# Sums of squares of the first expert's weights on TensorE, the last chunk's operands kept on chip, and a new sequence

## The chip, the cores and the metric

One core of a Trainium2 chip runs the whole program: TensorE (PE) with its weight loads (PEld), VectorE (DVE), ScalarE (ACT), GpSimd (POOL), and SyncE (SP), which issues nearly all DMAs. The metric is the device time of one execution in microseconds (us).

## What is computed

Causal attention with a decay bias over 4 x 8 heads, 576 positions of 64 elements, then two feed-forward stages ("experts") over the 2304 tokens:

```
scores = q k^T / 8 + min(-(cum_i - cum_j), 0), masked;  attn = softmax(scores) v
x  = attn, heads side by side                     # 2304 x 512
h  = x @ w_in;  x = (h - tanh(h)) @ w_out          # 512 -> 2048 -> 512
y  = ((x @ w_a) * (x @ w_b)) @ w_out2              # 512 -> 1536 -> 512
```

All inputs and the output are float32.

## The kernel before

**Split products.** PE multiplies float16. A float32 matrix is scaled by a power of two and split into a high and a low float16 half; a product of two matrices is three float16 products (high-high, high-low, low-high). The power of two comes from the sum of squares of the matrix: an ACT Square over the tile with an accumulator gives one sum per partition (tile `wac`), a matmul with a 128x128 matrix of ones (`ones16`) adds them over the partitions into a one-column result in the PSUM bank `pv`, and five tiny DVE instructions (`pow2`, first of them `p2n`) turn that into the scale `wsc` and its inverse. Then the high half is made by a scaled copy (`copy_scaled`, on any of ACT, DVE, POOL) and the low half by a multiply and subtract (`lo_part`, on DVE or POOL). `w_split` (L902) does all this for one weight tile of 128 x 1024.

**First expert.** Its weights lie in `w1`: 8 chunks of 256 hidden columns, each an in-tile and an out-tile, so 16 tiles. Tokens go through in nine blocks of 256. Block 0 runs with the float32 weights, as they are fetched; `w_split` then turns each of the 16 tiles into halves in place, and blocks 1 to 8 use the split weights. Attention units (two heads of one batch, part of the positions) run on the same engines, ahead of the block that needs them.

**Second expert.** Its 18 weight tiles are fetched and split when the last attention unit is done (their Square stays on ACT in both kernels). Tokens go in blocks of 512. From the second on, sums of quarters of the matrices save one product in eight: `seven` for the two inner products, and in the last three blocks `four_act`, `four_mm`, `four_out` for the outer one. `four_act` makes the operands of both halves (l = 0 and l = 1) of a block from one chunk c of six; those of l = 1 are stored to DRAM (`pb_d`, from the tile `sq`, tag sq4, one buffer) and loaded again (tile `x2f`, two buffers) when `four_mm` for l = 1 multiplies them. In the last block the chunks 4 and 5 of l = 1 are plain: no sums, into two banks of their own (`blk["plain"]`). `four_out(l)` combines the four accumulators of a half by copies and adds; for the last block's l = 1 it is called before those two plain chunks, and `plain_out` adds their result and stores the rows. `four_out` for both halves uses the tile `th`, of which there is one, and `g`, of which there are two.

**What sets the order.** Operations are recorded with their operands. The string `ORDER` then lists every operation in the order in which it is issued, three characters each: the operation's number and which of its possible engines takes it. Each engine executes its share strictly in that order and waits by semaphores for operands and buffers. A changed number of operations needs a new string, and the new one puts all operations in another order.

Of the kernel before, what the change touches and what calls it, by code (L numbers as in the profile page):

```python
# [37 lines left out]
    "AAMAAEAB0AAIAAQAAUAAAAAYABsAB4ABoABwAAcAAgAAkAAsAAwAA0ABEABJABNABSAAoAA4AA8ABAABVABZABkACEACAAB8ACIACMACQACYAQQAIkACUACc"  # L38
    "ACgAF0ADAAC0AFsACkAQUADKACwAIoAI0ADMAQYABgAIYAIUAIcADEAIgAIsAF9ACoAC4AFwADRAIwAF4ABcADUAPIAGAAPEAQcAPNAY4AI4AI8AJAAC8AQA"
    "AJIADYAJEAFoAY8AJMAJ4AJQACtADdAJwAPRAPUADgAJ8ADsAiAAJ1AEgAJUAEsAqEAKEAMcADkADoADwAPwAD0AEkAZAAMgAMkAD4AD8AEwAGEAhwAEoAJs"  # L40
    "AE0AERAEUAGKAMpAHMAHQAMwAiEAh4AGMAEYAEAAEcAE4AEEAE8AFCAJYAJdAGYAFRAFFAPYAZEAFUAGQAJgAGcAHUAEIAFYAFdAHYAHcAZMAFIAQEAKOAEM"
    "AFNAFgAMYAQIAGUAGgAQMAGkAKJAGoAHgAHkAG9APcAPkAYUAh0AHoAPsAGuAPgAH8AP0AGwAHAAHuAG0AZIAHEAh8AKBAHwAG5AHIAKQAKUAKYAKcAKgAH0"
    "AKkAJmAIAALQAFkAMuAM1AKoAQgALcAIEAP4AIIAYYAiQAKsAKyAM6AM8ALBAH5ALEAP8ALIAXwAK0ALgANIAJpALUALYALkANAARAANEAQwARQAlcAYcANM"
    "ANQALMAX0AX4AX8ALoAYgALsALyAK4AYAAK8AMBANUAYEAZQAL0AMEAIMANYANeAIRANtAN8AL4AL9AYIANwAOAAMIAiMAOIANhAUQAPoANkAYOAMMAiIAN0"
    "AYkAOEAjIAiUAOMAOQANpAiYAicAUYAikAigAOUAQkAN4AioAixAOYAMQAOeAOtAisAYoATwAOwAO0Ai9AOgAOkAQoAMVAlqAT4AO5AOoAO8AliAjAAQsAjV"
# [103 lines left out]
    "EVQEV8EUwEWcEKpEWgEVFEWBEWFEWwEWIEKsEVIEW8EWoEWMEVUEXAEYoEW0EVZEWQETMEYAEYIEVcEW4EWsEXEEXJEYMEYwEXNEXQEXVEVgEYsEZEEYFEXq"  # L149
    "EXsEYQEVkEXZEXwEXcEYgEY0EY8EYkEXiEY5EZIEZMEbUEZQEYcEZUEbMEbcEbIEYVEYZEbYEZBEXkEZYEZ9EbQEbgEVoEZcEZlEZtEZxEZpEZhEZ0EZ4EaB"  # L150
    "EX4EX8EX0EbkEbsEboEbwEb0EaIEb4EaMEb8EaZEcAEaVEcsEcwEc0EaQEaEEc4Ec8EdAEacEahEapEasEakEa1Ea4EawEa8EbAEcEEcNEcIEcREcZEcgEcU"
    "EccEcoEdYEdcEdhEclEdIEdNEdQ"
# [1895 lines left out]
```

## Time and profile before

| | us |
|---|---|
| three runs, median (lowest to highest) | 931.09 (930.62 to 933.18) |
| profiled execution, device time | 930.71 |
| its span, first to last instruction | 928.9 |
| DMA, whole span | 123.38 MB, 133 GB/s in the mean |

A busy share is an average over stages with different limits, so the rows below cut the span into stretches. "Idle" of an engine in a stretch is its length less the busy time. A timeline row begins with start and duration; a row with xN merges N instructions, from the first start to the last end; "[0.70 <-ACT qk]" says how long the engine stood idle before and what released it. Matmuls overlap in the array, so one takes longer than the distance to the next.

### The profile page before, as it was taken

The numbers are of one execution on the slowest core, as the hardware profiler recorded it, in microseconds if no ns is written. First come the engines' busy times: TensorE is split into PE (matmuls) and PEld (weight loads), VectorE is DVE, ScalarE is ACT, GpSimd is POOL, SyncE is SP. The second block draws the span as 40 slices with busy tenths as digits, with TensorE's granted clock in tenths as the row PEclk, the third lists the DMA queues.
The fourth block names the chain that finished last, engine by engine and source line by source line (L and its number), as shares of the span: only waits on it lengthen the run. The fifth ranks groups of instructions, "written<-read, shape, count | busy, mean of one in ns | idle before, by whom it ended". The sixth has DMA issues, their size and how long they took to land.

```text
span 928.9 us, 20616 instructions
## 1 busy us (share of the span) xinstructions
PE 881.3 (95%) x7650; PEld 647.6 (70%) x7650; DVE 805.7 (87%) x2011; ACT 574.1 (62%) x1136; POOL 346.1 (37%) x495
## 2 busy tenths in 40 slices
PE   1798899999999999999899999999999999999996
PEld 1565576766666666567566677777778888888884
DVE  8999999789999899997999999989798749864764
ACT  6999998668889888974998544433333323421310
POOL 2523356344544654552222310143322342344342
PEclk9999999999999999999999999999999999999998
DMA  8979976668999998975866300300211161123223
GB/s 204 304 214 238 231 123 124 113 154 171 206 165 174 193 179 167 208 137 161 308 206 189 84 24 1 69 2 1 47 54 53 60 185 65 62 72 112 72 68 115
DMA packets 260197, 123.38 MB, mean 133 GB/s; under 512 B 228544, under 2 KB 236976, under 8 KB 260096
## 3 DMA queue, kind: packets, MB, share of 16 engines
q1 hardware_dynamic: 259936, 121.79, 55.6%
q8 instruction: 60, 0.98, 0.4%
q14 instruction: 41, 0.34, 0.1%
q10 hardware_dynamic: 160, 0.26, 0.1%
HBM read 63.67 MB, written 19.03 MB: 89 GB/s over the span
## 4 chain that ended last, share of the span: by engine, by line
PE 47%; DVE 5%; issue 2%; DMA 1%; POOL 1%; ACT 0%; SPq 0%; POOLq 0%; DVEq 0%; ACTq 0%
PE h L647 16%; PE qk L647 12%; PE acc L647 11%; PE pv L647 8%; DVE w L647 1%; DVE x2f L647 1%; DVE g L647 1%; DMA x2f<-pb_d 0%; DMA out_dram<-x2f 0%; DVE a L647 0%; DVE ghl L647 0%; DVE sq L647 0%; DVE xf L647 0%; DVE h L647 0%; DVE th L647 0%
## 5 line engine op out<-in xcount | busy, mean ns | idle before, releaser
L647 PEld LDWEIGHTS <-w 128*128 128x128 f16 x3840 | 372.2, 98 | 67.0 <-issue 4.0
L647 PE MATMUL h<-xhl,w 128*128 128x256 f16 x2256 | 276.9, 273 | 2.4 <-DVE ghl L647 1.1
L647 PE MATMUL acc<-w,ghl 128*128 128x512 f16 (+1 forms) x1092 | 233.6, 358 | 0.9 <-DVE sq L647 0.9
L647 PEld LDWEIGHTS <-ghl 128*128 128x128 f16 x1290 | 123.6, 98 | 99.9 <-issue 4.8
L647 PE MATMUL h<-xf,w 128*128 128x256 f16 (+1 forms) x416 | 71.3, 310 | 0.0
L647 DVE CUSTOM_DVE_ANT_0 qk<-qk,caus,cs 128x384 f32<-128x384 f32 (+3 forms) x120 | 64.9, 555 | 2.8 <-PE qk L647 1.4
L647 PE MATMUL qk<-xf,w 128*128 128x256 f16 x432 | 55.2, 273 | 0.8 <-DVE xf L647 0.6
L647 PE MATMUL pv<-xf,w 128*128 128x256 f16 x432 | 55.0, 273 | 0.0
L647 ACT ACTIVATE g<-h 128x512 f32<-128x512 f32 x40 | 23.4, 592 | 48.8 <-PE h L647 27.0
L647 ACT ACTIVATE w<-w 128x1024 f32<-128x1024 f32 (+1 forms) x45 | 50.9, 1156 | 1.4 <-DVE w L647 1.4
L647 ACT ACTIVATE th<-h,xc 128x512 f32<-128x512 f32 x64 | 43.7, 683 | 9.5 <-PE h L647 7.4
L647 PE MATMUL qk<-qkT 128*128 128x128 f16 (+4 forms) x168 | 45.7, 316 | 3.7 <-ACT zs L647 3.1
L647 PE MATMUL qk<-kB,qB 67*128 67x128 f16 (+4 forms) x168 | 45.3, 313 | 3.9 <-ACT zs L647 2.2
L647 PEld LDWEIGHTS <-v 128*64 128x64 f16 x1440 | 37.7, 113 | 12.8 <-issue 10.8
L647 PEld LDWEIGHTS <-x2f 128*128 128x128 f16 x360 | 35.1, 98 | 7.1 <-DMA x2f<-pb_d 0.8
L647 DVE SCALAR_TENSOR_TENSOR h<-h,xc,th 128x512 f32<-128x512 f32 x48 | 36.0, 751 | 1.6 <-ACT th L647 1.6
L647 ACT ACTIVATE zs<-qk,nm 128x128 f32<-128x128 f32 (+1 forms) x64 | 30.2, 472 | 11.2 <-DVE nm L647 9.4
L647 DVE SCALAR_TENSOR_TENSOR ghl<-h,xsg,ghl 128x512 f16<-128x512 f32 x48 | 35.8, 746 | 1.4 <-ACT ghl L647 0.9
L647 DVE SCALAR_TENSOR_TENSOR a<-qk,sm,a 128x512 f16<-128x512 f32 (+1 forms) x56 | 35.2, 630 | 1.4 <-ACT a L647 1.0
L647 ACT ACTIVATE qk<-qk,nm 128x512 f32<-128x512 f32 (+1 forms) x56 | 31.7, 566 | 7.4 <-DVE nm L647 5.4
L647 ACT ACTIVATE sq<-qk 128x512 f32<-128x512 f32 x22 | 13.1, 594 | 37.4 <-PE qk L647 35.0
L647 PE MATMUL pv<-aT,v 128*64 128x128 f16 x960 | 34.5, 225 | 1.3 <-DVE aT L647 0.8
(367 smaller groups left out, 1872.0 us busy)
## 6 DMA issues: line engine op xcount, KB each, us to landing
w<-in_moe_w_out_dram SPq DMA_DIRECT2D x8, 1024.0 KB
pb_d<-sq SPq DMA_DIRECT2D x16, 448.0 KB
x2f<-pb_d SPq DMA_DIRECT2D x16, 448.0 KB
w<-in_moe_w_in_dram SPq DMA_DIRECT2D x6, 1024.0 KB
x_d<-sq SPq DMA_DIRECT2D x9, 512.0 KB
w<-in_moe_w_a_dram SPq DMA_DIRECT2D x4, 1024.0 KB
out_dram<-x2f SPq DMA_DIRECT2D x16, 256.0 KB
ws<-in_moe_w_out_dram SPq DMA_DIRECT2D x3, 1024.0 KB
```

The costliest lines, as they stand in the source:

```text
L647: return getattr(getattr(plan.nc, name), what)(*[real(a) for a in args], **{k: real(a) for k, a in kw.items()})
```

## The change

1. `w_split` takes a new path for the 16 tiles of the first expert (`GRAMS = 16`). The upper 16 bits of each float32 weight are read as bfloat16 (every second element). Eight matmuls of such a 128x128 piece with itself add up in PSUM to a 128x128 matrix, whose diagonal holds the sums of squares. One DVE instruction multiplies that by the identity `eyeh` and accumulates each row into `wac`. The matmul with ones then goes into a column of the same bank beside it. The ACT Square is gone for these tiles.
2. For the last chunk (c = 5) of the last block the operands of l = 1 are neither stored nor loaded; `four_mm` takes them from the tile where `four_act` wrote them.
3. `four_out` for the last block's l = 1 uses a free place in `w1` in place of `th` and `g`, makes the products `yy` of the two output scales itself and scales by them in one copy on any engine; `plain_out` reuses `yy`.
4. A new `ORDER`.

```
 ORDER = (
-    "AAMAAEAB0AAIAAQAAUAAAAAYABsAB4ABoABwAAcAAgAAkAAsAAwAA0ABEABJABNABSAAoAA4AA8ABAABVABZABkACEACAAB8ACIACMACQACYAQQAIkACUACc"
+    "ABkAB0AAAAAEAAIABwABoAB4AAQAB8AAMAAUAAYABsAAcAAgACAAAkAAsAAwAA0ABEABJABNAAoABRAA4ABVABaAQQAA8ABAACEACIACMAIoAIUACQACYACc"
...
+GRAMS = 16
...
+    def gram(flat, acc, g):
+        x = flat.bitcast(BF16)[:, 1::2]
+        n = flat.shape[1] // P
+        with pl.group():
+            for i in range(n):
+                y = x[:, i * P:(i + 1) * P]
+                pl.tensor.matmul(g, y, y, start=(i == 0), stop=(i == n - 1), skip_group_check=True)
+        pl.vector.tensor_tensor_reduce(
+            out=g, in0=g, in1=eyeh, scale=1.0, scalar=0.0, op0=ALU.mult, op1=ALU.add, accum_out=acc)
+
     def w_split(wf, dst, inv, junk):
...
-        pl.scalar.activation(out=junk, in_=wf, func=AF.Square, accum_out=acc)
         tot = bank("pv")
-        pl.tensor.matmul(tot[:, :1], ones16, acc.bitcast(BF16)[:, 1:2], start=True, stop=True)
-        pow2(tot[:, :1], 1, inv, sc)
+        if junk is None:
+            gram(wf.rearrange("p a b -> p (a b)"), acc, tot[:, 0:P])
+        else:
+            pl.scalar.activation(out=junk, in_=wf, func=AF.Square, accum_out=acc)
+        tot = tot[:, P:P + 1]
+        pl.tensor.matmul(tot, ones16, acc.bitcast(BF16)[:, 1:2], start=True, stop=True, skip_group_check=True)
+        pow2(tot, 1, inv, sc)
...
+        if many(blk, c) == 4 and c == C2 - 1:
+            return res
         pl.sync.dma_start(pb_d[(blk["nth"] - FOUR) * C2 + c][:, 0:2 * many(blk, c) * P], t, writes=[("pb", blk["nth"], c)])
...
-        if l:
+        if l and not (plain(blk, c) and c == C2 - 1):
...
     def plain_out(blk, ob):
         for i in (1, 0):
             g = blk["off"] // P + 3 - i
-            yy = new("moe", [P, 1], F32, "wac", 3)
-            small("tensor_tensor", out=yy, in0=y1[:, g:g + 1], in1=y2[:, g:g + 1], op=ALU.mult)
+            yy = blk["yy", i]
...
     def four_out(blk, l):
         z, y1_, y2_, x = blk["acc", l]
-        e = new("moe", [P, 512], F32, "th", 1, True)
-        f = new("moe", [P, 512], F32, "g", 2, True)
+        own = l and plain(blk, C2 - 1)
+        if own:
+            e, f = [w1[:, 14, i * 512:(i + 1) * 512].bitcast(F32) for i in range(2)]
+        else:
+            e = new("moe", [P, 512], F32, "th", 1, True)
+            f = new("moe", [P, 512], F32, "g", 2, True)
...
-            out_rows(blk["off"] // P + 2 * l + 1 - i, r, r, not (l and plain(blk, C2 - 1)))
+            if own:
+                g = blk["off"] // P + 3 - i
+                blk["yy", i] = new("moe", [P, 1], F32, "wac", 3)
+                small("tensor_tensor", out=blk["yy", i], in0=y1[:, g:g + 1], in1=y2[:, g:g + 1], op=ALU.mult)
+                copy_scaled(r, r, blk["yy", i])
+                continue
+            out_rows(blk["off"] // P + 2 * l + 1 - i, r, r)
...
-                junk = new("moe", [P, 1024], BF16, "sq", 2).rearrange("p (a b) -> p a b", a=n)
+                junk = None if i < GRAMS else new("moe", [P, 1024], BF16, "sq", 2).rearrange("p (a b) -> p a b", a=n)
```

On PE, in block 0, the first weight sum behind the first expert products, before (`h` and `acc` are float32 expert products, `pv_742` is the bank for the sum, `wac_717` the sums that ACT wrote):

```order
L647 MATMUL h_591<-xf_451,w_0_154 128x256 x2
L647 LDWEIGHTS ones_69
L647 MATMUL pv_742<-wac_717,ones_69 128x1
L647 MATMUL h_591<-xf_451,w_0_154 128x256 x2
L647 MATMUL acc_4_761<-w_0_154,g_730 128x512 x2
L647 MATMUL acc_4_764<-w_0_154,g_730 128x512 x2
```

The same place now; `w_0_141` is the weight tile itself, `wac_750` the sums that DVE writes:

```order
L648 MATMUL h_686<-xf_454,w_0_141 128x256 x2
L648 LDWEIGHTS w_0_141
L648 MATMUL pv_738<-w_0_141 128x128
...
L648 MATMUL h_686<-xf_454,w_0_141 128x256 x2
L648 LDWEIGHTS ones_69
L648 MATMUL pv_738<-wac_750,ones_69 128x1
L648 MATMUL h_624<-xf_454,w_0_141 128x256 x4
L648 MATMUL acc_4_789<-w_0_141,g_761 128x512 x2
```

The pair of LDWEIGHTS and MATMUL on `w_0_141` stands eight times; two expert products lie between it and the matmul with ones.

On DVE the reduction stands between them, in a row of other work (`v`, `qk`: operands of attention units; `g`: the step behind the tanh; `p2n`: the first of the five tiny ones):

```order
L648 TENSOR_SCALAR qk_708<-raw_245,sc_655 128x4x64
L648 SCALAR_TENSOR_TENSOR qk_708<-raw_245,sc_655,qk_708 128x4x64 x2
L648 ISA pv_738,wac_750<-pv_738,eyeh 128x128
L648 ISA wac_750 128x1
L648 SCALAR_TENSOR_TENSOR v_752<-raw_245,sc_655,v_752 128x16x64
L648 SCALAR_TENSOR_TENSOR g_761<-h_686,th_756 128x512
L648 TENSOR_SCALAR p2n_766<-pv_738 128x1
```

Before, only `p2n` stood there; the reduction and the read of its accumulator (`ISA`, twice) are new on DVE.

At the end of DVE's queue, before (`x2f_13117` are the rows of l = 0, `x2f_13132` those of l = 1, `acc_20` the plain banks):

```order
L647 TENSOR_TENSOR x2f_13117<-qk_12489,th_13074 128x256
L647 TENSOR_SCALAR x2f_13117<-x2f_13117,y_0_1749,y_0_8637 128x512
L647 TENSOR_TENSOR th_13127<-th_13127 128x256
L647 TENSOR_TENSOR x2f_13132<-g_13130 128x256
L647 TENSOR_TENSOR g_13130<-g_13130,th_13127 128x512
L647 TENSOR_TENSOR x2f_13132<-qk_12955,th_13127 128x256
L647 TENSOR_TENSOR x2f_13132<-pv_12954,g_13130 128x512
L647 TENSOR_SCALAR x2f_13132<-x2f_13132,y_0_1749,y_0_8637 128x512
L647 SCALAR_TENSOR_TENSOR x2f_13132<-acc_20_13085,wac_8639,x2f_13132 128x512
L647 SCALAR_TENSOR_TENSOR x2f_13132<-acc_20_13078,wac_8641,x2f_13132 128x512
```

And now (`x2f_13204` is l = 1, `x2f_13238` is l = 0):

```order
L648 TENSOR_TENSOR w_0_141<-w_0_141 128x512
L648 TENSOR_TENSOR x2f_13204<-x2f_13204,w_0_141 128x256
L648 TENSOR_TENSOR x2f_13204<-qk_13074,w_0_141 128x256
L648 TENSOR_TENSOR x2f_13204<-pv_13073,w_0_141 128x512
L648 TENSOR_SCALAR x2f_13204<-x2f_13204,wac_8907 128x512
L648 TENSOR_TENSOR x2f_13238<-g_13201 128x256
L648 TENSOR_TENSOR g_13201<-g_13201,th_13206 128x512
L648 TENSOR_TENSOR x2f_13238<-qk_12647,g_13201 128x512
L648 TENSOR_TENSOR x2f_13238<-qk_12648,th_13206 128x256
L648 TENSOR_SCALAR x2f_13238<-x2f_13238,y_0_1886,y_0_8755 128x512 x2
L648 SCALAR_TENSOR_TENSOR x2f_13204<-acc_20_13209,wac_8907,x2f_13204 128x512
L648 SCALAR_TENSOR_TENSOR x2f_13204<-acc_20_13216,wac_8785,x2f_13204 128x512
```

The half l = 1 now stands ahead of l = 0, and only the two closing additions of the plain products remain behind both.

## Rows read from the trace of the kernel before

**Rows 1.** busy us of each engine over the span (share, instructions), from the page
```profile
PE 881.3 (95%) x7650; PEld 647.6 (70%) x7650; DVE 805.7 (87%) x2011; ACT 574.1 (62%) x1136; POOL 346.1 (37%) x495
```

**Rows 2.** stretches: length, busy us of PE, PEld, DVE, ACT, POOL, granted clock, DMA share, GB/s
```profile
0.00:17.40 17.40, 0.54 (x5) 0.46 (x5) 13.28 (x49) 10.28 (x22) 3.34 (x14) 1.00 0.80 188
17.40:40.00 22.60, 14.88 (x109) 9.25 (x109) 22.17 (x91) 21.91 (x59) 12.33 (x24) 1.00 1.05 273
40.00:115.00 75.00, 68.18 (x363) 42.97 (x362) 72.70 (x219) 71.52 (x137) 22.71 (x39) 0.98 0.95 240
115.00:441.00 326.00, 323.57 (x3295) 217.13 (x3295) 294.78 (x868) 261.99 (x556) 158.40 (x241) 1.00 0.85 162
441.00:475.00 34.00, 30.17 (x210) 19.68 (x208) 32.83 (x74) 33.58 (x47) 7.34 (x8) 1.00 0.74 261
475.00:900.00 425.00, 423.56 (x3514) 342.43 (x3513) 354.28 (x690) 173.10 (x317) 135.36 (x165) 1.00 0.24 74
900.00:921.00 21.00, 20.44 (x164) 15.72 (x162) 12.02 (x23) 1.72 (x3) 5.13 (x6) 1.00 0.28 86
921.00:929.00 8.00, 0.00 (x0) 0.00 (x0) 3.66 (x6) 0.00 (x0) 1.49 (x2) 0.63 0.37 120
```

**Rows 3.** waits of PE: engine, tile, releaser: us in total, times, longest
```profile
PE pv L647 <- ACT sq L647: 11.3, 4, 7.6
```

**Rows 4.** groups of ACT instructions, the weights' Square: xcount | busy us, mean ns | idle
```profile
L647 ACT ACTIVATE sq<-w 128x1024 bf16<-128x1024 f32 x15 | 15.9, 1059 | 0.3 <-DVE w L647 0.3
...
L647 ACT ACTIVATION_READ_ACCUMULATOR sq<-w 128x1 f32 x15 | 3.0, 199 | 0.0
```

**Rows 5.** timeline of ACT and PE at the start: start us, us, operation [idle before]
```profile
16.15 1.06 ACT L647 ACTIVATE sq<-w 128x1024 bf16<-128x1024 f32 x1
...
18.34 0.26 PE L647 MATMUL qk<-kB,qB 67*128 67x128 f16 x1 [0.70 <-ACT qk L647]
```

**Rows 6.** timeline of PE, 128x128 products at 38, 45 and 58 us
```profile
38.19 1.16 PE L647 MATMUL qk<-eyeh,a 128*128 128x128 f16 x6
...
45.17 0.50 PE L647 MATMUL qk<-eyeh,a 128*128 128x128 f16 x6
...
58.45 0.22 PE L647 MATMUL qk<-qkT 128*128 128x128 f16 x1
```

**Rows 7.** groups of weight loads, those of f32 weights
```profile
L647 PEld LDWEIGHTS h<-xf,w 128*128 128x128 f32 x128 | 23.7, 194 | 6.3 <-issue 2.2 <-DVE w L647 0.4 <-ACT xf L647 0.3
```

**Rows 8.** timeline of DVE, first score reductions
```profile
19.18 0.34 DVE L647 CUSTOM_DVE_ANT_0 qk<-qk,caus,cs 128x128 f32<-128x128 f32 x1
19.45 0.13 DVE L647 DVE_READ_ACCUMULATOR2_ANT nm<- 128x1 f32 x1
19.45 0.48 DVE L647 CUSTOM_DVE_ANT_0 acc<-acc,caus,cs 128x256 f32<-128x256 f32 x1
```

**Rows 9.** groups of DVE instructions: score reduction of 128x128, copy of 128x256
```profile
L647 DVE CUSTOM_DVE_ANT_0 qk<-qk,caus,cs 128x128 f32<-128x128 f32 x32 | 11.1, 349 | 0.1
...
L647 DVE TENSOR_SCALAR xf<-pv,inv 128x256 f32<-128x256 f32 x9 | 4.3, 478 | 1.0 <-PE pv L647 0.9 <-ACT xtail L647 0.2
```

**Rows 10.** timeline of PE in block 0, a wait for ACT
```profile
79.08 0.22 PE L647 MATMUL qk<-qkT 128*128 128x128 f16 x1 [2.12 <-ACT zs L647]
```

**Rows 11.** stretch behind that wait, columns as in rows 2
```profile
80.00:82.00 2.00, 2.00 (x3) 0.33 (x1) 2.00 (x6) 2.00 (x4) 0.21 (x1) 0.50 1.25 246
```

**Rows 12.** timeline of the tail, last products to last DVE instruction
```profile
917.68 2.75 PE L647 MATMUL acc<-w,x2f 128*128 128x512 f16 x12
...
919.35 0.60 ACT L647 ACTIVATE th<-h 128x512 f32<-128x512 f32 x1 [10.73 <-DVE x2f L647]
...
919.90 5.55 SPq L647 DMA_DIRECT2D out_dram<-x2f  x4
...
924.19 0.75 DVE L647 SCALAR_TENSOR_TENSOR x2f<-acc,wac,x2f 128x512 f32<-128x512 f32 x1 [0.20 <-POOL x2f L647]
```

**Rows 13.** timeline of PE, first run of split products in block 1
```profile
115.03 3.33 PE L647 MATMUL h<-xhl,w 128*128 128x256 f16 x29 [0.33 <-DVE xhl L647]
```

More of the change, by code (lines that the diff above doesn't have):

```diff
@@ L42 @@
[L42 to L45, printed above, removed]
@@ L150 @@
[L150 to L152 removed]
+    "ABkAB0AAAAAEAAIABwABoAB4AAQAB8AAMAAUAAYABsAAcAAgACAAAkAAsAAwAA0ABEABJABNAAoABRAA4ABVABaAQQAA8ABAACEACIACMAIoAIUACQACYACc"
+    "ACUAClAF0AC0ACgADAAFsAIkAQUAI0ACwABgAIgACoAIYAIcADJADMAQYADEAIsAF4AIwAI4AF8AC4ABcADUAFwAGAADYADRAPEAPIAQcAPNAC8AQAAFoAI8"
@@ new lines @@
+    "APRAZAAJAAJIAJEAJMAJ4ACtAZEAZIAJQADdAjAAJwAPUADgAMcAJsAJ8ADsADkADoAEsAJUAJ1AKEADwAD0AZMAMkAGEAEgAEkAEoAMgAD4AD8AEwAE0AER"
+    "AJgAPwAGKAHMAMpAEUAGMAEYAEAAHQAE4AEEAHUAE8AFCAZQAJYAEcAFRAjEAMwAJdAFUAFFAPYAGQAQEAQIAEIAZYAGYAMYAKOAi4AGcAGgAiwAFYAFdAZc"
+    "AHYAHcAi0AEMAGUAFIAFNAQMAGkAHgAKJAGoAHkAi8AFgArEAPcAG9AGuAHoAH8AHsAGwAHAAQgAKBAG0AG5AIAAHEAPsAP0AJmAHIAKQAKcAHxAMuALQAKU"
+    "AKYAKgAKkAPkAFkALcAIEALUALYAZUAH0AH5AP4AKoAPgAYYAM1AKsALBAYcAM6AM8AIIAYgAjQALEARQANIALIAKyAK0AK4AkIAK8ALMAP8AQwAYkANAANE"
@@ new lines @@
+    "ARAAYoALgALkAXwAX0AX4ANMAJpAX8APoAYsANQAYwAY0AYAALoALsAjIAYIAIMALyAMBANUAMEAL1ANYAIRAYMAN8ANtAjMAOAAOIAMIAMMANeAL4ANwAmc"
+    "AOMAL8AUQAYEAN0AjUANhAYSAjYANkANpAOEAUYAjcAOQAN4AjkAjoAMQAOUAjgAjxAOYAOeAQkAjsAj9ATwAOtAOwAO0AMUAOgAOkAQoAOoAkMAT4AmqAO5"
+    "AkVAkYAO8APAAT8AQsAmwAZoAmhAmkAmsAZsAkAAT0AUAAkEAm0AUEAZwAkRAZ0AQ0AQ4AUcAkgAYUAUUAQ8AUgAUkAY6AREARgAo8AZ4AUIAaAAaEAUMARI"
+    "Aj0AaQAUwAkcAaUAU0AkoArIAj5AY8ARMAm8ARwAaYAacAklAagAaoARVAZgAU4AU8ARYAVAAa4AlgAk4AksAasAa8AbAAm4ApAAo2AbEAUoAUsAkwAbIAk8"
@@ L153 @@
+    "EdREdcEdYEdsEbYEdlEbdEblEboEbsEbgEbwEb0Eb4Eb9Ed8EeEEeAEeQEeJEeUEeZEeM"
 )
@@ L1725, in four_out, with out_rows @@
             r = ob[:, i * 512:(i + 1) * 512]
-            out_rows(blk["off"] // P + 2 * l + 1 - i, r, r, not (l and plain(blk, C2 - 1)))
+            if own:
[5 more added lines that the diff above has]
+            out_rows(blk["off"] // P + 2 * l + 1 - i, r, r)
         return ob
-    def out_rows(g, ob, src, store=True):
+    def out_rows(g, ob, src):
         kw = dict(out=ob, in0=src, scalar1=y1[:, g:g + 1], scalar2=y2[:, g:g + 1], op0=ALU.mult, op1=ALU.mult)
@@ L1734, in out_rows @@
             pl.vector.tensor_scalar(**kw)
-        if store:
-            out_store(g, ob)
+        out_store(g, ob)
     def out_store(g, ob):
```

211 lines of the change are left out of this document (104 added, 107 removed).

## The prediction

> **What bounds the kernel now.** I read the page's busy times first: PE is busy 881.3 of 928.9 us [rows 1], so 47.6 us of idle time on PE is all that any edit can win unless PE's own work shrinks. Then I cut the span into stages at the places where the other engines' load changes [rows 2]. The reader is to see in them that PE's idle time is not spread evenly. Until 17.4 us PE has next to nothing (16.9 us idle), from 17.4 to 40 it is fed by the first attention units (22.60 - 14.88 = 7.7 idle), from 40 to 115, the first block of the first expert, it idles 6.8. In all 326 us from 115 to 441 it idles only 2.4, in the hand-over to the second expert 3.8, from 475 to 900 only 1.4. PE ends at 920.4, and the last 8.5 us are the chain after it. Second thing to see: from 17.4 to 115 DVE is busy 94.9 and ACT 93.4 of 97.6 us, so there these two set the pace and PE is third; from 115 on PE sets it. The Square instructions that the change removes all lie before 115. So the two places to price are the stretch up to 115 us and the tail. The list of PE's waits names the Square directly [rows 3]: 11.3 us in four waits, but these are waits at the start, for the loads' sums too, and only one of the four is for a weight.
>
> **Removed from ACT.** Sixteen times a Square of 1.06 us and its accumulator read of 0.20 [rows 4]: 20.2 us, all between 16 and 114 us. By the order, fifteen copies that DVE or POOL made move onto ACT in exchange, which I price between 0.48 us (the xf copy [rows 9], 256 wide) and 1.06 (the Square, 1024 wide): 7.2 to 15.9 given back, so ACT is lighter by 4 to 13. I take 8, near the middle. The first Square stood in the start: it holds ACT from 16.15 to 17.4, and the first pair of score matmuls waits behind it for kB until 18.34 [rows 5]. Without it kB can come a good microsecond earlier, but the same order puts a Gram product, its DVE step and the ones matmul ahead of that pair. I count 0.5 to 1 us gained there.
>
> **Added to PE.** 16 x 8 = 128 pairs of LDWEIGHTS and a 128-column matmul. The nearest rows are the six 128x128 products of attention weights and the identity [rows 6]. At full clock six take 0.50 us from first start to last end; with the 0.22 us of one by itself that is (0.50 - 0.22) / 5 = 56 ns from start to start, and 83 ns if the whole 0.50 is shared out. At 38 us the same six took 1.16, up to 193 ns each, although the granted clock of that stretch reads 1.00 [rows 2]; I take the row, not the clock. Three Gram products stand before the first expert matmul: 24 pairs, 2.6 to 4.6 us, in a stretch where PE idles 7.7. Thirteen stand in block 0: 104 x 56 = 5.8 us (8.6 at 83 ns), against 6.8 us of idle. So the addition fits, at 56 ns with 1 us to spare, but only if the idle time really closes up. What the rows do not show is an operand with a stride of two elements, for the weight load and the moving side. Upper bound: the f32 weight load takes 194 ns [rows 7], which as a pitch makes 104 x 138 = 14.4 us more. Lower bound: none below the 56, since columns do not get fewer. I take 56, because the products in rows 6 have the same shape. The SBUF page of the Trainium skill (SBUF — State Buffer, section Door 1: The DMA port swizzle) lets a bf16 pattern stride by up to eight elements at full rate, by which the stride costs 0; no row here shows it.
>
> The TensorE page of the Trainium skill (TensorE: Matmul & The Clock Gate, section Back-to-back issue gap) gives about 81 ns for a sustained 128-column matmul with its weight load in a real kernel, and 56 ns for the isolated gap. The transposes here run at 56, so the trace sides with the shorter figure; by 81 the thirteen would cost an estimated 104 x 81 = 8.4 us. It makes a rival below.
>
> **Added to DVE.** Sixteen masked reductions of 128x128 from PSUM with an accumulator read. The score reduction is the same instruction on the same shape: it lasts 349 ns [rows 9], and the timeline shows the next one starting 0.27 us after it, with the 0.13 us read under it [rows 8]. So 0.27 to 0.48 each; for the fifteen that precede the last tanh step of block 0 that is 4.1 to 7.2 us. Against it the order shows a net of eight DVE instructions fewer there, of 0.35 to 0.48 us each [rows 9]: 2.8 to 3.8. Net +0.3 to +4.4; I take +1, near the start-to-start row. DVE has 0.4 + 2.3 = 2.7 us of idle in that stretch, and part of its and PE's waits are for an ACT that is now lighter: one wait of 2.1 us for an exponential on ACT at 79 us, after which the granted clock stands at 0.50 for 2 us [rows 10, 11]. So the end of block 0 moves by -1 (start) + 1 (DVE) = 0. Bounds: -3.1 (that wait gone, 2.1, and the half-clock stretch, which loses 1.0 of its 2 us) and +4.4.
>
> New waits: each ones matmul waits on PE for DVE's reduction, where it waited for ACT before. PE's queue is in order, so the expert products behind it wait too. In the order most of them have two to eight products between the Gram product and the ones matmul, and DVE needs 0.35 us plus the rest of what it is in the middle of. I cost that at nothing beyond the idle time counted; the rival below takes it seriously. PSUM's pv bank is held for longer, from Gram to scale; its other users are units of attention and norms, in turn with it in the same queue.
>
> **115 to 900.** The same products in another order. 7.7 us of idle PE in 785; I see no term and put 0, within 1.5 either way. DVE is nearly full only in 441 to 475, where the second expert's weights still have their squares on ACT.
>
> **The tail.** The store and reload of the last chunk's operands go. PE idles nowhere between 900 and 920.4 (20.44 busy in 20.43 [rows 2, 12]), so the load is hidden and its removal by itself is worth 0. What gains is the order behind it. Before, the last products end at 920.43, but the first copy of the l=1 half on ACT could start only at 919.35, 10.73 us idle until DVE had released the tile that both halves share; its chain of adds follows and the last DVE instruction ends at 924.94, 4.5 us after PE [rows 12]. Now that half has tiles of its own and stands ahead of the other on DVE; behind PE's last product only the last of the two closing additions is left, 0.75 us, and at most both. 4.5 - 0.75 to 4.5 - 1.7 is 2.8 to 3.7 us won. Against it, the four output rows that were stored from 919.90 on are now all stored in the last 2 us. I take -2.6, bounds -3.5 and 0.
>
> **Sum.** Profiled execution 930.71 (span 928.9): 0 + 0 - 2.6 = 928.1. The median of the runs, 931.09, is 0.38 above the profiled one; with it 928.5. The likeliest case's own range is 925.5 to 931.5.
>
> **Rivals.**
> - ACT held more than I think. For: the 2.1 us wait and the slow clock behind it [rows 10, 11], ACT 95.4% busy up to 115. Against: DVE is as full and gets more. Worth 3.1 more: 925.4.
> - DVE sets block 0, and PE waits at the ones matmuls: slower. For: DVE at 97% there, and a third hand-over per weight (PE to DVE to PE to DVE). Place: the thirteen ones matmuls of block 0. Price: DVE's net at +4.4 in place of +1, and one reduction of 0.27 us [rows 8] waited out at each, 3.5: 928.5 + 3.4 + 3.5 = 935.4. Against: ACT's share of the waits goes. It decides the sign once the two together pass 2.6.
> - The pairs cost 83 ns, weight loads not hidden under 128 columns: 104 x 27 = 2.8 us more on PE, less the 1.0 to spare: 930.3 to 931.3. The section of the TensorE page named above says this. Rows 6 speak against it.
> - The stride doubles the weight load as f32 does: up to 14.4 more, 941.9. Against it speaks only that the element is no wider.
> - The tail's gain does not come, because the crowded stores take its place: 931.1.
>
> **How the numbers follow.** Two runs of this kernel can be told apart from about 0.3%, 2.8 us: faster means below 928.3, slower above 933.9. Forecast 0.54 (its centre lies on the edge: 0.30 faster, 0.24 same), ACT's relief 0.13 (faster), DVE and hand-overs 0.18 (0.16 slower, 0.02 same), 83 ns 0.08 (same), stride 0.05 (slower), tail not won 0.02 (same). Faster 0.43, same 0.36, slower 0.21. The range 924.5 to 935.0 leaves out the stride, half of the DVE case and a little of the first rival.
>
> **What would show it.** Eight Gram pairs in about 0.6 us from first start to last end at full clock; no Square of weights before 115; the first full run of split products of block 1 at 115 us, as now [rows 13]; the last DVE instruction within 2 us of PE's last product. Wrong if the pairs take over 0.8 us, if PE waits for the sums tile over 3 us in block 0, or if the first split product comes after 118.

## The result, and the profile after

The changed kernel took 940.03 us (median of 3 runs, 939.56 to 940.36) where the kernel before took 931.09: a ratio of 1.0097, 95% interval 1.0078 to 1.0117. I had forecast 928.5 and a range up to 935.0. Two later measurements of the same kernel, on two chips and with more runs, gave 935.48 (1.0063, 1.0052 to 1.0075) and 936.83 (1.0067, 1.0053 to 1.0082). It is slower in all three, by 5 to 9 us.

The busy line of the page answers to [rows 1]: ACT has lost 10 us and PE has gained 10.

```profile
PE 891.8 (95%) x7778; PEld 657.9 (70%) x7778; DVE 804.3 (86%) x2045; ACT 563.7 (60%) x1103; POOL 355.3 (38%) x507
```

The same view of stretches as [rows 2], of the changed kernel. A stretch from 115 to 124.6 us stands between, because block 0 now ends 9.6 us later, and the cuts behind it lie 9 us later than before:

```profile
0.00:17.40 17.40, 0.74 (x6) 0.66 (x7) 12.56 (x44) 9.71 (x21) 3.19 (x13) 1.00 0.78 186
17.40:40.00 22.60, 15.14 (x121) 10.73 (x118) 20.83 (x94) 19.58 (x53) 11.88 (x22) 1.00 1.06 273
40.00:115.00 75.00, 70.17 (x413) 46.04 (x411) 66.56 (x211) 61.47 (x114) 20.45 (x38) 0.95 0.90 223
115.00:124.60 9.60, 7.88 (x69) 5.34 (x68) 8.68 (x34) 6.96 (x14) 2.19 (x4) 1.00 0.79 165
124.60:450.00 325.40, 320.24 (x3272) 214.98 (x3272) 291.39 (x866) 254.92 (x542) 172.02 (x252) 1.00 0.81 158
450.00:484.00 34.00, 30.49 (x210) 19.87 (x209) 33.03 (x70) 32.58 (x45) 6.34 (x9) 1.00 0.78 277
484.00:909.00 425.00, 423.20 (x3503) 341.33 (x3502) 354.80 (x708) 173.82 (x312) 128.11 (x158) 1.00 0.24 75
```

From 40 to 115 us ACT and DVE are less full than before (61.5 and 66.6 of 75 us, where they had 71.5 and 72.7), and still the block ends later. The list of instructions on tile h puts the first split product of block 1 at 124.1 us, and at 114.4 in the kernel before. The two lines are of the changed kernel and of the kernel before; after the count stand the shortest, median and longest in ns, then the first and last start in us.

```profile
L648 PE MATMUL h<-xhl,w x105: 269/273/283, 124.1 to 145.0; 128*128 128x256 f16 x105
```

```profile
L647 PE MATMUL h<-xhl,w x150: 270/272/273, 114.4 to 145.0; 128*128 128x256 f16 x150
```

That is 9.7 us in block 0, more than the whole loss. The last product ends at 932.97 in place of 920.43, so the middle has lost another 2.8, and the tail gives back 3.0: from the end of the last product to the end of the span there were 8.5 us, now 5.4. The rows of the tail that answer to [rows 12]:

```profile
926.85 0.60 ACT L648 ACTIVATE th<-acc 128x512 f32<-128x512 f32 x1 [1.70 <-PE acc L648]
930.22 2.75 PE L648 MATMUL acc<-w,sq 128*128 128x512 f16 x12
932.27 3.22 SPq L648 DMA_DIRECT2D out_dram<-x2f  x3
932.62 1.40 DVE L648 SCALAR_TENSOR_TENSOR x2f<-acc,wac,x2f 128x512 f32<-128x512 f32 x2
```

DVE's last addition ends 1.05 us after PE. The longest wait of PE in block 0 is in its timeline between 72 and 93 us (in brackets the idle time before the instruction and what ended it; `zs` are the exponentials of an attention unit, `aT` its transposed weights):

```profile
71.92 0.62 PE L648 MATMUL pv<-w 128*128 128x128 bf16 x8
...
81.66 0.22 PE L648 MATMUL qk<-qkT 128*128 128x128 f16 x1 [1.00 <-ACT zs L648]
...
86.40 1.12 PE L648 MATMUL pv<-aT,v 128*64 128x128 f16 x17 [2.52 <-DMA aT<-a]
...
88.08 1.01 PE L648 MATMUL pv<-w 128*128 128x128 bf16 x8 [0.24 <-ACT xf L648]
88.89 3.72 PE L648 MATMUL acc<-w,g 128*128 128x512 f32 x4
```

A Gram product of eight pairs takes 0.62 us at full clock, as forecast; only the first three, before 40 us, take 1.01 each, although the granted clock of their stretches reads 1.00. But PE waits 2.52 us for a transposing transfer of attention weights, and behind the wait the same eight take 1.01 and four products of the second layer 3.72 instead of 1.9. The granted clock of that stretch is 0.50, the lower of the two levels (1.2 GHz), and it stays there until about 92.7 us.

```profile
86.00:88.00 2.00, 1.44 (x19) 1.11 (x19) 1.70 (x3) 1.25 (x3) 0.14 (x1) 0.50 1.37 221
```

The theories that I took into the experiments: A, the Grams themselves lengthen block 0; B, the new sequence does, by its waits and transfers; and for both, that ACT's relief is worth something in return.

### The profile page after: what moved, and what is told of

The parts are those of the page before. It is cut to its first block, busy times and chain, and to the rows that moved or that the text cites. A ratio compares the mean times of both kernels' runs of the same rounds, so it can differ in the third digit from the quotient of the medians.

```text
span 938.4 us, 20849 instructions
## 1 busy us (share of the span) xinstructions
PE 891.8 (95%) x7778; PEld 657.9 (70%) x7778; DVE 804.3 (86%) x2045; ACT 563.7 (60%) x1103; POOL 355.3 (38%) x507
## 4 chain that ended last, share of the span: by engine, by line
PE 48%; DVE 4%; DMA 2%; issue 1%; ACT 1%; POOL 0%; DVEq 0%; POOLq 0%; ACTq 0%; SPq 0%
PE h L648 16%; PE qk L648 12%; PE acc L648 11%; PE pv L648 8%; DVE w L648 1%; DMA x2f<-pb_d 1%; DMA w<-in_moe_w_out_dram 1%; DVE a L648 0%; DMA x_d<-sq 0%; DVE g L648 0%; DVE h L648 0%; DVE sq L648 0%; DVE x2f L648 0%; POOL w L648 0%; DVE qk L648 0%
## 5 line engine op out<-in xcount | busy, mean ns | idle before, releaser
L648 PEld LDWEIGHTS <-w 128*128 128x128 f16 (+1 forms) x3960 | 381.6, 98 | 82.6 <-issue 9.8
L648 POOL TENSOR_TENSOR a<-zs,a 128x128 f16<-128x128 f32 (+1 forms) x44 | 32.2, 732 | 3.7
```

The costliest lines, as they stand in the source:

```text
L648: return getattr(getattr(plan.nc, name), what)(*[real(a) for a in args], **{k: real(a) for k, a in kw.items()})
```

## Experiments

Each run was timed beside the kernel before on the same chip (930.15 to 930.68 us there). "First split product" is the first h<-xhl,w, as in the two lines above.

**Parts alone.** The first four take the change apart. In `tail_only` the source has no Grams, and only the steps from the last chunk on are those of the changed kernel.

```
-GRAMS = 16
+GRAMS = 0
-ORDER: new sequence
+ORDER: old sequence up to the last chunk, then the new tail
```

> The kernel before with the tail of the change alone: last chunk's operands on chip, the other half of the output rows finished first; no Grams, and the old sequence up to the last chunk. In the trace after, 5.4 us lie from the end of the last matmul to the end of the span, in the one before 8.5. If the tail's gain stands by itself, the time is 931.1 - 3.0 = 928 us (927.3 to 928.9). If it came only with the rest of the new sequence, or is given back by the products of the last chunk standing in another order, 930.5 to 932 us.

Measured: 927.34 against 930.26, ratio 0.9975 (0.9964 to 0.9987), 2.9 us. The tail's gain stands by itself, at the size forecast.

```
 tot = bank("pv")
+for i in range(8): matmul(tot[:, 0:P], w_i, w_i)
 matmul(tot[:, P:P + 1], ones16, acc)
```

> The kernel before with the sixteen groups of eight 128x128 products added on PE, right in front of each ones matmul and in the same bank, and read by nobody: the Squares stay on ACT, VectorE does nothing more, the sequence is the old one. It prices the PE work alone. Theory A: PE's idle time in block 0 (14.5 of 97.6 us) is not to be had for it, and 13 groups of 0.46 us add 6 us: 936 to 938 us, first split product at 120 to 122. Theory B: the groups fit into the idle time ahead of the ones matmuls: 930.5 to 932.5 us, first split product at 115 to 116.5.

Measured: 932.32, ratio 1.0025 (1.0015 to 1.0035), first split product at 117.1. So 2.1 us of the 6 come through; the rest does close up idle time. At 79 and at 84 us PE waits for ACT in both kernels, and the product behind the second wait starts at 83.94 with nine of the groups recorded ahead of it, at 83.90 without them: in these traces nothing came through up to there. The two lines of this run, then the second one of the kernel before (its first is [rows 10]):

```profile
79.18 0.22 PE L647 MATMUL qk<-qkT 128*128 128x128 f16 x1 [1.65 <-ACT zs L647]
...
83.94 0.22 PE L647 MATMUL qk<-qkT 128*128 128x128 f16 x1 [1.65 <-ACT zs L647]
```

```profile
83.90 0.22 PE L647 MATMUL qk<-qkT 128*128 128x128 f16 x1 [0.65 <-ACT zs L647]
```

In the next two, one kernel's way of taking the sums is put into the other's sequence.

```
-ORDER: Square of weights 1, 3 to 12, 15 on ACT
+ORDER: Gram on PE as early as the pv bank is free, its sum on DVE three steps later
```

> The kernel before with 12 of the 16 sums of squares (weights 1, 3 to 12 and 15) taken by PE as in the change, each put as early as the one pv bank is free in the old sequence, the product with the identity on VectorE three places behind; the rest of the sequence and the tail stay old. Theory A: 11 groups of 0.46 us after the first expert matmul, and PE's waits for VectorE's sums, lengthen block 0 by 5 to 8 us: 936 to 939 us. Theory B: ACT's relief and the groups cancel, first split product at 114 to 117, 930 to 933 us.

```
-ORDER: Gram on PE, sum on DVE
+ORDER: Square on ACT, as far ahead of its ones matmul as in the old sequence
```

> The changed kernel with one part undone: the sixteen sums of squares are again ACT Squares, each put as many places ahead of its ones matmul as in the kernel before; everything else keeps the new sequence and the new tail. Theory A (the Grams themselves lengthen block 0: 13 of them at 0.46 to 0.62 us on a PE that has no idle time to spare, and the pv bank that each holds): block 0 gets 6 to 8 us back, the first split product of block 1 stands at 117 to 118.5 us and the time is 932 to 934 us. Theory B (the new sequence is what costs: its transposing transfer of aT that PE waits 2.5 us for, the stretch at the lower clock behind it, the start 1 us later): the first split product stays at 122 to 126 us and the time at 937 to 941 us.

Measured: 946.27 (1.0175, 1.0161 to 1.0189) with the first split product at 127.5, and 949.57 (1.0196, 1.0174 to 1.0218; five runs between 944.2 and 950.3) at 133.0. Both are slower than either kernel, and both theories' numbers are missed. With Grams in the old sequence PE waits at nine of the Grams, 11.2 us in all, and the two longest that name DVE are of two kinds:

```profile
54.70 0.73 PE L648 MATMUL pv<-w 128*128 128x128 bf16 x8 [3.87 <-DVE p2b L648]
...
82.55 0.62 PE L648 MATMUL pv<-w 128*128 128x128 bf16 x8 [1.47 <-DVE inv_in L648]
```

The second waits for the one pv bank, which DVE's `p2n` (82.36 to 82.50) reads last. At the first the bank was free 3 us before; what ends then on DVE, at 54.64, is the step that puts together the float32 words of a weight:

```profile
51.53 0.15 DVE L648 TENSOR_SCALAR p2n<-pv 128x1 f32<-128x1 f32 x1
...
53.43 1.21 DVE L648 SCALAR_TENSOR_TENSOR w<-w 128x1024 int32<-128x1024 int32 x1
```

So this Gram stood ahead of its weight, as far as the names in the trace tell.

With Squares in the new one PE waits for the Squares, in the list of its waits between 17 and 140 us:

```profile
PE pv L648 <- ACT sq L648: 8.7, 4, 3.1
```

Each sequence fits the durations that it was written for, and a swap of one kind of instruction under it tells little of that instruction.

**Moves that seemed to win.** The next four were compared with the 940.0 of the first measurement.

```
-for i in range(n):          # n = 8, scale 1.0
+for i in range(1):          # scale 8.0
```

> The changed kernel, its sequence untouched, with one 128x128 product in each Gram group in place of eight (the sum over the first eighth of the columns, times 8, so the scales and the output differ a little); the product with the identity on VectorE, the ones matmul and every wait stay. It takes 0.40 of the 0.46 us out of each group. Theory C (in the new sequence PE's own work is the bound of block 0, so each Gram counts in full): 13 groups x 0.40 = 5.2 us, 934.5 to 935.5 us, first split product near 119.5. Theory D (PE waits in block 0 for what others bring, and the Grams lie beside that, as 16 idle groups cost only 2 us in the old sequence): 938 to 940 us, first split product at 122.5 to 124.5.

```
-SP: load q, load v, load s, load k
+SP: load s, load q, load v, load k
```

> The changed kernel with one step moved: SyncE issues the load of s first, ahead of the two loads that the new sequence puts before it (1.78 us after the change, 1.25 before). If the 1.0 us by which the new sequence's first chain on VectorE is late (4.70 against 3.73) passes to the end: 938.5 to 939.3 us against 940.0. If the first products then wait for the loads of q, k and v instead: 939.7 to 940.5.

```
-SP: load w (1 MB), transpose aT<-a
+SP: transpose aT<-a, load w (1 MB)
```

> The changed kernel with one step moved: on SyncE the 1 MB load of w at 79.0 us goes behind the transposing transfer aT<-a that stands after it, so that this does not land behind the load. Theory D: PE's wait of 2.5 us at 84 us goes, and with it the stretch at the lower clock that follows it (about 3 us): 934.5 to 936.5 us. Theory C, or if the wait moves on to the weight that is now late: 939 to 941 us.

```
-ORDER: new sequence throughout
+ORDER: new up to step 800, old up to the last chunk, new tail
```

> The changed kernel with its new sequence only as far as the end of block 0 and in the tail; from there to the last chunk the order is that of the kernel before. After the change PE was idle 10.4 us in the 800 us behind its first split product, before 7.7. If that is the new sequence of the middle: 936.8 to 938 us. If it comes from the later start of the loads, or from chance: 939 to 940.5 us.

Measured: 935.10, 935.68, 937.67 and 934.84 us. Each seems to win, but `old_middle` shows that something is off: its instructions up to block 0's end are those of the changed kernel, and yet its first split product comes 4.2 us sooner, without the wait for aT. So the changed kernel itself was measured again.

> The changed kernel as it is, beside the other runs on one chip, since its sequence up to block 0's end gave a first split product at 124.1 us in one trace and at 119.9 in another whose order differs only behind that place. If the loss is the kernel's own: 939 to 941 us, and PE's wait for aT with the slow stretch is in the trace again. If it hangs on how the transfers happen to fall: 934 to 938 us, or runs that lie over 3 us apart.

Measured: 935.48 (935.08 to 937.06), with the first split product at 119.5. The wait for aT is 1.69 us here, and the clock stays at its upper level behind it. Its timeline of PE, and the stretch that answers to the one at 0.50 above:

```profile
84.56 0.66 PE L648 MATMUL pv<-aT,v 128*64 128x128 f16 x17 [1.69 <-DMA aT<-a]
...
86.25 1.93 PE L648 MATMUL acc<-w,g 128*128 128x512 f32 x4
```

```profile
86.00:88.00 2.00, 2.00 (x12) 0.97 (x10) 2.00 (x8) 2.00 (x4) 1.06 (x3) 1.00 1.37 218
```

In the first profile SyncE spent 3.81 us on issuing the transfer ahead of it, and 2.98 here; the 1 MB load that stands between the two transposing transfers went out at 79.01 and 77.15 us:

```profile
74.73 3.81 SPq L648 DMA_TRANSPOSE aT<-a  x1
79.01 0.37 SPq L648 DMA_DIRECT2D w<-in_moe_w_in_dram  x1
79.49 2.31 SPq L648 DMA_TRANSPOSE aT<-a  x1
```

```profile
73.71 2.98 SPq L648 DMA_TRANSPOSE aT<-a  x1
77.15 0.37 SPq L648 DMA_DIRECT2D w<-in_moe_w_in_dram  x1
78.09 1.79 SPq L648 DMA_TRANSPOSE aT<-a  x1
```

By and large PE waits longer the longer the two transfers take to issue: 2.52 us with 3.81 and 2.31 in the first trace, 1.69 with 2.98 and 1.79 here, 0.88 with 2.11 and 1.65 in a third measurement (`after_third`, below), not at all with 2.16 and 1.23 in `old_middle`. `gram_one_pair`, with 3.69 and 1.22, waits 2.03, and `s_first`, with 3.08 and 1.98, 1.80. In the third measurement:

```profile
75.47 2.11 SPq L648 DMA_TRANSPOSE aT<-a  x1
```

```profile
85.50 0.66 PE L648 MATMUL pv<-aT,v 128*64 128x128 f16 x17 [0.88 <-DMA aT<-a]
```

The first two measurements lie 4.5 us apart, and their first split products 4.6. Of these, 3.6 come from this wait and the slow stretch behind it. The other 1.0 is there before it (81.66 against 80.65 for the product that waits for `zs`): 0.35 from the start, 0.66 from 41 to 46 us, where four f32 products of `h` take 1.43 us in the first trace, 1.08 in the second and 1.82 in the third, at a granted clock that reads 1.00 in all three. The third trace is 1.8 us behind the second at its first split product without any slow stretch behind the wait. The mean granted clock points the same way for the runs that were not profiled: 0.995 to 0.996 in the three of the first measurement, 0.997 to 0.999 in the eleven later ones.

So the gains of the four moves over 940.0 show nothing by themselves. Against the kernel before on their own chip they stand at 1.0048, 1.0055, 1.0075 and 1.0045, where the changed kernel has 1.0063 and 1.0067 on its later two; every one of these intervals overlaps theirs. Moving the load did remove the wait for aT, as meant, but the next wait came in its place, for ACT's xf, with the slow clock behind it again. ACT's xf is late because ACT first waits 1.50 us for the very load that was moved:

```profile
85.39 1.13 ACT L648 ACTIVATE w<-w 128x1024 int32<-128x1024 uint16 x1 [1.50 <-DMA w<-in_moe_w_in_dram]
```

```profile
86.92 0.95 PE L648 MATMUL pv<-w 128*128 128x128 bf16 x8 [2.70 <-ACT xf L648]
87.67 3.31 PE L648 MATMUL acc<-w,g 128*128 128x512 f32 x4
```

> The changed kernel with the three moves of the last runs at once: s loaded first, the 1 MB load behind the transposing transfer, the old order between block 0's end and the last chunk. By themselves they measured 4.4, 2.4 and 5.2 us less than 940.0. If they add: 928 us. If the first two (and the third's share in block 0) remove the same wait and slow stretch: start 1.0 to 2, wait and slow stretch 4 to 5.5, middle 1.5, so 931.5 to 934 us, which leaves the Grams' 5 to 6 us less the tail's 3.

Measured: 935.48, on the chip of the second measurement, where the changed kernel took 935.48 as well. The three moves together win nothing there: in the traces the middle takes 807.0 us from the first split product to the last product, against 808.3, but that first split product comes at 121.8 against 119.5, behind a wait of 2.26 us for the same xf.

**What ACT's relief is worth.**

```
-scalar.activation(out=junk, in_=wf, func=AF.Square, accum_out=acc)
+acc = one
```

> The kernel before without the sixteen Squares of the first expert's weights: the ones matmul sums a constant instead, so the scales of these weights are fixed and the output is another; nothing takes the Squares' place and the old sequence stays. It is the most that relieving ACT of them can give in the old sequence (the forecast took 7 to 16 us of ACT's time as given back elsewhere). If ACT's load bounds block 0 (71.5 of 75 us busy): first split product at 107 to 111 us, 922 to 926 us. If PE's own work and the in-order waits bound it: 111.5 to 115 us, 927 to 930.5 us.

Measured: 930.49 against 930.15, ratio 1.0001 (0.9988 to 1.0014), first split product at 114.0. Taking all sixteen Squares away, with nothing in their place, is worth nothing that 1.3 us of interval would show. From 60 to 80 us ACT is 3 us emptier than in the kernel before, and DVE as full:

```profile
60.00:80.00 20.00, 17.69 (x70) 10.90 (x68) 19.94 (x61) 16.42 (x34) 5.00 (x9) 1.00 1.09 290
```

```profile
60.00:80.00 20.00, 17.66 (x69) 10.90 (x68) 19.95 (x63) 19.46 (x41) 5.34 (x9) 1.00 1.00 302
```

PE's wait for ACT's zs, the one that I took as a sign of a late ACT [rows 10], is still there. In the kernel before ACT works without a gap from 67.8 us to the end of that wait, two Squares among its work:

```profile
68.27 1.05 ACT L647 ACTIVATE sq<-w 128x1024 bf16<-128x1024 f32 x1
...
71.81 1.09 ACT L647 ACTIVATE sq<-w 128x1024 bf16<-128x1024 f32 x1
```

Without them ACT waits in their place, for DVE, for a load and for PE. From 74.3 us on it works without a gap on what stood there before too, and the exponentials end half a microsecond earlier, no more:

```profile
70.77 0.37 ACT L646 ACTIVATE zs<-qk,nm 128x128 f32<-128x128 f32 x1 [0.72 <-DVE a L646]
...
72.08 1.17 ACT L646 ACTIVATE w<-w 128x1024 int32<-128x1024 uint16 x1 [0.85 <-DMA w<-in_moe_w_out_dram]
...
74.33 0.60 ACT L646 ACTIVATE th<-h 128x512 f32<-128x512 f32 x1 [0.44 <-PE h L646]
...
78.04 0.36 ACT L646 ACTIVATE zs<-qk,nm 128x128 f32<-128x128 f32 x1
...
78.54 0.22 PE L646 MATMUL qk<-qkT 128*128 128x128 f16 x1 [2.09 <-ACT zs L646]
```

Since DVE is full from 60 to 100, it was the next suspect:

```
-DVE: three shifts and two copies of w, three copies of a, one of xf
+ACT: the same nine
```

> The old sequence without the sixteen Squares (a constant is summed instead; the output is another), which alone measured no difference from the kernel before, and with nine instructions that VectorE issues between 53 and 108 us given to ACT, which the Squares left 14 us emptier: three shifts of words of w (0.69 us each), two copies w<-w,wsc (0.75), three copies of a and one of xf (0.47). That takes 5.5 us off VectorE and puts some 7 on ACT. If VectorE is what bounds block 0 in the old sequence (busy 39.95 of the 40 us from 60 to 100): first split product at 109.5 to 112.5 us, 926 to 928.5 us. If neither ACT nor VectorE bounds it but PE and the waits of its own order: 929.5 to 931.5 us.

Measured: 933.69, ratio 1.0037 (1.0024 to 1.0049), first split product at 116.2. Slower, which neither theory has: PE's waits for ACT's zs from 40 to 120 us grew from 2.4 to 4.8 us, and with the last of them, of 2.46 us, the clock fell to 0.50 until 88. That ACT's load is not the bound does not make it free to take more at these places. Whether DVE bounds block 0 is not settled by it.

**The ledger on one chip.** With the changed kernel beside them, on the chip on which `tail_only` had run:

> The changed kernel as it is, to stand on the same chip as the three beside it: the two runs so far gave 940.0 and 935.5 us, 4.5 us apart, and in the traces those lie between 80 and 93 us. 935 to 941 us; near 940 only if the trace shows the slow stretch behind the wait for aT, near 935.5 only if it doesn't.

```
-gram(wf, acc, tot[:, 0:P])
+acc = one
```

> The changed kernel without the sixteen Gram groups and without the products with the identity on VectorE: the ones matmul sums a constant, so the scales of the first expert's weights are fixed and the output is another; the new sequence stays. The counterpart in the old sequence measured no difference from the kernel before, and with the new tail it would stand at 927.5 us. If the Grams and their waits are the whole loss: 926.5 to 929 us, first split product near 114.5. If the new sequence costs by itself: 931 to 935 us, first split product at 117 to 119.5.

```
-for i in range(n): matmul(g, y_i, y_i)          # scale 1.0
+for i in range(2 * n): matmul(g, y_i, y_i)      # i modulo n, scale 0.5
```

> The changed kernel with each Gram group run over its eight blocks twice (the sum times one half, the same value). If PE's own work is the bound wherever a Gram stands, 13 more groups of 0.46 us pass in full: 6 us over the changed kernel beside it. If about a third of it comes through, as with the idle groups in the old sequence (2.1 of 6 us): 2 us over it. One pair in place of eight measured 935.1 us on another chip, which by the first would put the changed kernel at 940 there, by the second at 937.

`old_middle_again` is the kernel of `old_middle`.

> The changed kernel with the old order between block 0's end and the last chunk, once more, now with the changed kernel on the same chip. If the new sequence's middle costs by itself: 1.5 to 2.5 us under the changed kernel. If it does not, and the 934.8 us of the first run were the other chip: within 0.8 us of it.

| kernel | us | against the changed kernel | first split product |
|---|---|---|---|
| before | 930.68 | -6.2 | 114.4 (first profile) |
| changed (after_third) | 936.83 | | 121.3 |
| no Grams and no sums, new sequence | 933.27 | -3.6 | 116.6 |
| Grams twice | 943.46 | +6.6 | 129.6 |
| old middle | 934.77 | -2.1 | 120.5 |

The Grams with their sums cost 3.6 us. A second helping of 6 us of PE work costs 6.6 in the median, where the first idle helping in the old sequence cost 2.1. Its four runs fall into pairs: 941.5 and 942.1 with a mean granted clock of 0.999 and 1.000, so 4.6 and 5.2 us over the changed kernel, and 944.9 and 945.1 with 0.997. So most of the second helping is PE's work itself, and the rest goes with a lower clock. The view of stretches of the changed kernel on this chip shows why, PE has nothing left to give from 60 to 80.

```profile
60.00:80.00 20.00, 20.00 (x113) 13.96 (x111) 18.90 (x60) 17.26 (x32) 4.18 (x8) 1.00 1.05 301
```

The new sequence without any sums stands at 933.27, where the old one without any sums, with the new tail, would stand at 930.7 - 2.9 = 927.8; that kernel was not run, the figure puts `no_squares_old_order` and `tail_only` together. So the sequence by itself costs 5.5, by the three intervals certain to some 2 us: 2.1 in the middle, and by difference 3.4 up to the end of block 0, where the two traces without sums show 116.6 against 114.0. That 3.6 + 5.5 - 2.9 gives the 6.2 us measured is no check, since the 5.5 is itself a difference.

The 2.1 of the middle rests on two medians whose runs overlap (933.96 to 937.45 against 935.89 to 937.68). The traces bear it out: from the first split product to the end of the last product the middle takes 806.6 us in the mean of the seven with the old order in block 0 and the middle (804.9 to 808.4), 806.9 in the three with the old order only there, and 808.6 in the nine with the new one (807.8 to 809.4).

**The version that the runs point to.**

```
-ORDER: new sequence, GRAMS = 16
+ORDER: old sequence, load of s first, new tail, GRAMS = 0
```

> The version that the runs point to: the old sequence with its Squares and the new tail (927.3 us), and the load of s issued first instead of second (1.25 us becomes 0.73). If the half microsecond at the start passes on: 926.5 to 927 us. If the first products wait for ACT's Squares of q and k instead (7.6 us of waits at 8.5 to 16.3 us): 927 to 928 us. Either way below the 930.3 of the kernel before.

Measured: 926.54 against 930.15, ratio 0.9965 (0.9953 to 0.9977). It is faster than both kernels. Its interval overlaps that of `tail_only`, so what moving the load of s adds is not shown.

## Why the prediction was wrong

The step that failed is the end of block 0: "-1 (start) + 1 (DVE) = 0", with bounds of -3.1 and +4.4. It measured +9.7 in the first profile, +5.1 and +6.9 in the two others. The sum put the Grams' time on PE at nothing, as hidden in idle time, and had no term for the new order; the runs show 3.6 us for the Grams with their sums and 5.5 for the order. By its parts:

- Start, -0.5 to -1: the first score matmul comes 1.25 us later instead (18.63 against 17.38), the one with kB 0.7 later (19.06 against 18.34). The new sequence loads s third in place of second, DVE's first chain starts 1.0 us later (4.70 against 3.73), the Gram takes 1.01, and PE waits 0.45 for the sum at 18.60. The prediction named the Gram, its DVE step and the ones matmul ahead of that pair but took too little off for them, and did not see the later load. The first lines are of the changed kernel, the last of the kernel before:

```profile
17.15 1.01 PE L648 MATMUL pv<-w 128*128 128x128 bf16 x8 [0.30 <-DVE p2n L648]
18.60 0.16 PE L648 MATMUL pv<-wac,ones 128*128 128x1 bf16 x1 [0.45 <-DVE wac L648]
18.63 0.27 PE L648 MATMUL qk<-qkT 128*128 128x128 f16 x1
```

```profile
17.38 0.27 PE L647 MATMUL qk<-qkT 128*128 128x128 f16 x1
```

- PE, 5.8 us of Grams "if the idle time really closes up": the duration was right, eight pairs in 0.62 us, (0.62 - 0.22) / 7 = 57 ns each; the stride costs nothing, and the rivals of 83 ns and of the f32 load are out. The three before 40 us took 1.01 each, 3.0 together, within the 2.6 to 4.6 given for them. By the TensorE page of the Trainium skill (TensorE: Matmul & The Clock Gate, section Back-to-back issue gap) a pair in a real kernel would take about 81 ns; the measured 57 decide against it here. They agree with the SBUF page of the Trainium skill (SBUF — State Buffer, section Door 1: The DMA port swizzle), by which the stride is free. The condition failed in part: 2.1 us come through in the old sequence, and in the new one 3.6 with the sums. A sum of idle slices does not say which of them lie in front of a wait that ends at a fixed time.
- ACT lighter by 8, within 4 to 13: from 17.4 us to block 0's end ACT was busy 93.4 us before and 88.0 after, so 5.4. But the relief is worth nothing, which `no_squares_old_order` shows. I had read a busy share of 95% as a pace, and a wait named after ACT as a sign of it. Two Squares did stand in ACT's unbroken work before that wait, but where they went ACT waited for DVE, a load and PE instead.
- DVE +1: 94.9 us before, 96.1 after up to the end of block 0, so +1.2. The amount was right, but not what was made of it: the end of block 0 was to move by DVE's net, and in the first profile it moved by 9.7 us while DVE was busy 96.1 of 107.2 us, no longer full.
- New waits at the ones matmuls, costed at nothing: PE's waits for the sums' tile come to 1.7 us in four waits from 17 to 120 us. Small, and the rival that put 3.5 us there had the wrong place, though its time (935.4) lies near the two later measurements; that is luck.
- What I had no term for is the new sequence: 5.5 us by the ledger. For the middle I had put 0 within 1.5, and 2.1 is just outside. In block 0 I took the order as given, and priced only the instructions that come and go.
- The transfer that arrives late and the 0.50 clock behind it, 3.6 of the 4.5 us by which the first measurement is longer than the second: in no case of mine. That the kernel before has the same kind of wait in the same place (2.12 us, then the clock at 0.50 [rows 10, 11]) was in front of me, but I used it only as something that could go.
- Tail, -2.6 within -3.5 and 0: -3.0 in the first profile, -2.9 alone. Right, with its mechanism: 1.05 us from PE's last product to DVE's last addition.

Left open: which engine or chain sets the end of block 0 in the old sequence, since neither a lighter ACT nor a lighter DVE moved it forward; what in the new order of block 0 costs its share of the 5.5 us; why the transposing transfer ahead took between 2.1 and 3.8 us to issue in one program; and how much of the 3.6 us is PE's products and how much the reductions and waits. A mended new sequence that also fits DVE and the pv bank was not tried.

## What to carry to other kernels

An engine that is 95% busy is worth relieving only if what the bound waits for then really comes earlier, and the engine does not wait for others in the place that came free, as ACT did here; leaving the instruction out with nothing in its place is one run and tells it at once. When a change comes with a newly written order, price the order as a term of its own, and separate it by leaving the disputed work out under both orders, not by forcing it into the order made for the other. And measure the changed kernel again beside every experiment that is meant to mend it: four moves here seemed to win 2.4 to 5.2 us because they were compared with a run made at another time.

## What the runs showed of the hardware

A bf16 product whose two operands are every second element of f32 words runs at the pitch of a dense one: eight pairs in 0.62 us, and sixteen in 1.08, which is 58 ns for each further pair, where six f16 products of a dense operand had 56 [rows 6]. The line is of `grams_twice`.

```profile
52.71 1.08 PE L648 MATMUL pv<-w 128*128 128x128 bf16 x16
```

In the traces of the kernel before and of the changed kernel the same work takes up to twice as long until 42 to 46 us as later, though the granted clock reads 1.00: in `after_again` two runs of four f32 products of `h`, the second behind the change:

```profile
41.34 1.98 PE L648 MATMUL h<-xf,w 128*128 128x256 f32 x4
...
43.51 1.08 PE L648 MATMUL h<-xf,w 128*128 128x256 f32 x4
```

One program, with fixed queues, differed by 4.5 us between two measurements; in the traces a wait of PE for a transfer was 2.52 us in one and 1.69 in the other, and the granted clock behind it 0.50 and 1.00. Waits of 2.03 (`gram_one_pair`), 2.52 and 2.70 us (`transpose_first`) in this place were followed by the lower clock; waits of 1.69 and 1.80 (`s_first`) were not, and one of 2.26 (`new_mended`) was not either. The length of one wait does not tell: behind a wait of 1.25 us the clock fell in `grams_twice`, behind 2.09 us for `zs` it fell in `tail_s_first` and did not in `tail_only`.
